# Letting the list of a fused attention and feed-forward kernel place the pooled sums on either of two engines

## The chip, the cores and the metric

The kernel runs on one core of a Trainium2 chip. The metric is the device time of one execution in microseconds (us); lower is better. The engines named below are TensorE (PE, matrix products; PEld is its weight load), VectorE (DVE), ScalarE (ACT), GpSimd (POOL) and SyncE (SP, which issues most DMA transfers). Each engine works through its own instructions in the order in which the program issued them, and an instruction that waits holds back those behind it.

## The reference

Per batch of 8, with 8 heads, 576 tokens and 64 columns a head (float32):

```python
q_d, k_d, v_d = (t.reshape(B, H, S // 4, 4, D).mean(axis=3) for t in (q, k, v))
out_up = np.repeat(softmax(scale * q_d @ k_d.T) @ v_d, 4, axis=2)      # pooled attention
mask = abs(pos[:, None] - pos[None, :]) < 4
out_local = softmax(where(mask, scale * q @ k.T, -1e9)) @ v            # local attention
x = (out_up + out_local).transpose(0, 2, 1, 3).reshape(B, S, H * D)
xn = (x - mean) / sqrt(var + 1e-6) * g_ln                              # over 512 columns
out = x + relu(xn @ w_ch1) @ w_ch2                                     # 512 -> 2048 -> 512
```

The weights come as 64-bit floats.

## The kernel before

**Feed-forward part.** The 4608 tokens are cut into 9 chunks of 512. TensorE visits every chunk twice: in the first stage with 5 of 8 pairs of weight columns (`wide`, L1228, and `down`, L1299), in the second with the other 3 (`product`, L1218, and `down`). Every operand is split into a high and a low part (`halved`: ScalarE copies the high part, L407; VectorE subtracts, L413), and three products make one of full precision. Between the two products ScalarE takes the ReLU (L1236) and VectorE the low rest (`hl`, L1243 and L1285), which also frees the PSUM bank of the first product.

**Attention part.** It runs beside the first stage. For each batch `pooled(b)` makes two halves of four heads (number i = 2b + half). For q, k and v of a half there are two loads into a staging tile (`raw4q` is q of i = 4; L819 on SP's queue; only 2 staging tiles, `NSTG`) and a sum of four tokens by two additions in `pool4` (L832 over 72x512 and L833 over 72x256). Batch 0 has its own path. After the sums TensorE transposes (`turn_qk`, L880), ScalarE copies (L889, L893), TensorE makes the scores (L907), VectorE the row maxima (L911, L912), ScalarE the exponentials (L920), TensorE transposes them (L926) and multiplies by v (L943), VectorE divides (L962), and `keep` (L968) writes the result to a DRAM tile `ud` by two DMAs from GpSimd's queue. The local attention works on 40 windows (`local`, L553 to L788), whose q and k loads (L566) are issued by SP or, for later windows, by ScalarE. `norm(i)` then adds both: `plus` (L1026) is two DMAs from GpSimd's queue that read `ud` and add into the window's tile `xl`; then VectorE takes the statistics (`stats`, L1049), GpSimd the inverse root (L1055), VectorE normalizes (L1059), GpSimd writes `xl` to DRAM (L1096), TensorE transposes (L1067), and ScalarE scales (L1090).

**Order.** Nothing of this order is fixed by hand. Each step is a task of `Plan` with an engine, a duration, what it depends on, a due time and the buffers that it takes and gives back. `Plan.order` builds one list: it repeatedly takes, over all engines, the task that can start first, within 0.5 us the one due first. A task may have a second engine (`alt`) with a duration and an added wait. The instructions are issued in the list's order, so the list decides what stands ahead of what on every engine. An error of the list's times is no error of the result: the chip's waits still hold, but an instruction that stands too early in its engine's queue blocks those behind it.

For a task that depends on a DMA task the list knows a landing time (`t.lag`). It is added to the time at which the later task may start only under this condition:

```python
x.open = max(x.open, t.end + (t.lag if t.eng == "SP" or set(x.opts) != {t.eng} else 0.0))
```

So it is not added where both tasks are on GpSimd alone, which holds for `keep` followed by `plus`. `plus` has 2 * 0.56 = 1.12 us in the list. `G1` is the gap in due time between the four pairs of heads of batch 1's pooled attention; from batch 2 on the gap is `ROUND / NPAIR`. Until the first product, idle slots of TensorE are filled with dummy products (L216).

Of the kernel before, what the change touches and what calls it, by code (L numbers as in the profile page):

```python
# [22 lines left out]
class Plan:  # L23
# [18 lines left out]
    def add(self, eng, dur, fn, deps=(), due=0.0, take=(), give=(), lag=None, ahead=1e9, alt=None, kb=0, n=1, more=0.1, late=None):  # L42

        opts = {eng: (dur, fn, 0.0)}
        if alt is not None:
            opts[alt[0]] = alt[1:]
        t = SimpleNamespace(
            n=len(self.tasks), opts=opts, dur=dur, deps=[d for d in deps if d is not None],
            due=due, take=take, give=give, lag=lag, ahead=ahead, open=0.0, waits=0, eng=None, fn=None, kb=kb, pieces=n, more=more,
            late=late if late is not None else self.late if eng == "SP" else 0.0,  # L50
        )
        self.tasks.append(t)
        return t

    def order(self):
# [40 lines left out]
        while left:  # L96
# [48 lines left out]
                free[room] = sorted(free[room] + [t.end + t.lag] * n)  # L145
            for x in then.get(t.n, ()):
                x.waits -= 1
                x.open = max(x.open, t.end + (t.lag if t.eng == "SP" or set(x.opts) != {t.eng} else 0.0))
                if not x.waits:
                    for e in x.opts:  # L150
                        ready[e].append(x)
# [6 lines left out]
def attention_then_ffn(  # L158
# [159 lines left out]
    AHEAD = 45  # L318
    U_SPARE = 4
    NEARLY, EARLY = 2, 0  # L320
    G1 = 6
    W2_LATER = 7.0
    W_LEAD = 4.0
    HALT = 1.0
# [13 lines left out]
    def act(n, sbuf=False):  # L338
        return (0.155 if sbuf else 0.14) + n / 1430.0
# [212 lines left out]
    def local(i):  # L552
# [44 lines left out]
        for src, nm in () if own else ((q, "q"), (k, "k")):  # L597
            if by_pe:

                def turn(nm=nm):  # L600
                    p = psa(f"l{nm}{i}")
                    x.p[nm] = p
                    for pr in range(NPAIR):
                        nc.tensor.transpose(
                            p[:, pr * P : (pr + 1) * P],
                            x.raw[nm][:, 2 * pr : 2 * pr + 2].rearrange("p h d -> p (h d)"), ident,
                        )

                def turn_out(nm=nm):
                    t = unit([P, NPAIR, P], f"l{nm}t{i}")  # L610
                    nc.scalar.copy(t.rearrange("p c t -> p (c t)"), x.p[nm])
                    setattr(x, nm + "t", t)

                t = add("SP", 1.33, lambda src=src, nm=nm: load_rows(src, nm), (), due - 12.0, take=U,
                        lag=LAT, kb=360, n=2, more=1.0, ahead=AHEAD)
                t = add("PE", 0.43, turn, (t,), due - 8.0, take=A, give=U)
                turned.append(add("ACT", act(512), turn_out, (t,), due - 8.0, take=U, give=A))
            else:

                def turn(nm=nm):  # L620
                    t = unit([P, H, 64], f"l{nm}t{i}")
                    nc.vector.transpose(
                        t.rearrange("p h j -> p (h j)"), x.raw[nm].rearrange("p h j d -> p (h j d)")
                    )
                    setattr(x, nm + "t", t)

                ts = []
                for jb in range(2):
                    ts.append(add("SP", 2.0, lambda src=src, nm=nm, jb=jb: load_blocks(src, nm, jb, nc.sync), ts,
                                  due - 14.0, take=() if jb else U, lag=LAT, kb=200, n=4, more=0.8, ahead=AHEAD,  # L630
                                  alt=("ACT", 3.2, lambda src=src, nm=nm, jb=jb: load_blocks(src, nm, jb, nc.scalar), LATER) if i >= ALSO else None))
                turned.append(add("DVE", dve(512), turn, ts, due - 8.0, take=U, give=U))
        if own:

# [146 lines left out]
        for h2 in range(2):  # L781
            t = add("DVE", 0.28, lambda h2=h2: inverse(h2), (tv,), due)
            outs.append(
                add("DVE", dve(256) * (1 if by_pe else 2), lambda h2=h2: divided(h2, "DVE"), [t] + outs, due,
                    take=() if h2 else U, give=A,
                    alt=("ACT", (4 if by_pe else 8) * act(64), lambda h2=h2: divided(h2, "ACT"), 0))
            )
        local_out[i] = x, outs  # L788

# [11 lines left out]
    def pooled_half(b, hg):  # L801
# [8 lines left out]
        for nm, src in (("v", v),) if own else (("q", q), ("k", k), ("v", v)):  # L810
            for half in range(2):
                key = (nm, half)
                due = pooled_at(b, 2 * hg) - (8.0 if nm == "v" else 14.0)

                def load(src=src, key=key):
                    half = key[1]
                    raw = work.tile([P, 1024], F32, tag="stg", bufs=NSTG, name=f"raw{i}{key[0]}{half}")
                    raw = raw[:GH].rearrange("p (h e) -> p h e", h=4)
                    nc.sync.dma_start(  # L819
                        raw,  # L820
                        src[b, 4 * hg : 4 * hg + 4, half * S // 2 : (half + 1) * S // 2, :]
                        .rearrange("h (g r) d -> g h (r d)", r=FACTOR),
# [13 lines left out]
                if own:  # L836
# [23 lines left out]
                    "DVE" if by_dve else "POOL", dve(512) + dve(256) if by_dve else 2.1,  # L860
                    (lambda key=key: pool4(key, nc.vector)) if by_dve else pool4, [t, lastg.vd[hg] if nm == "v" else None] + ready.get(nm, []),
                    due, take=U if half == 0 and nm != "v" else (), give=STG,
                )
                ready.setdefault(nm, []).append(t)
        for pr in range(2):
# [147 lines left out]
    def norm(i):  # L1013
# [88 lines left out]
            lastup["own"] = t  # L1102
            t = kept = add("DVE", dve(512), keep_x, [t] + outs, due - 1.0, give=A)
        else:
            t = kept = add("POOL", 2 * BEGUN, plus, ud_done[b] + outs, due - 4.0, lag=LAT, kb=400, n=2, more=0.6)
        t = add("DVE", 1.1, stats, (t,), due - 1.0)
        t = add("POOL", 0.52, rstd, (t,), due - 1.0)
        t = add("DVE", 0.46, normed, (t,), due, take=U, ahead=12.0)
# [357 lines left out]
```

## Time and profile before

| | us |
|---|---|
| median of 3 runs | 1030.08 |
| lowest and highest | 1027.56, 1035.27 |
| the profiled execution | 1034.97 |
| its span, first to last instruction | 1033.2 |
| mean granted TensorE clock in it | 0.997 of 2.4 GHz |

The profiled execution is one of its own and lies near the upper end of the runs; 1.8 us of its time lie outside the span. Start times below are from the start of the span. In brackets behind an instruction stands how long its engine had been idle before it, and what ended that.

### The profile page before, as it was taken

The page shows a single profiled execution, that of the slowest core. Times are in us where ns is not written, and L with a number is a line of the kernel's source. Part 1 is how long each engine was busy: PE and PEld are TensorE (multiplying, and loading weights), DVE is VectorE, ACT ScalarE, POOL GpSimd, SP SyncE. Part 2 cuts the span into 40 slices and gives each one's busy share as a digit, 9 for nine tenths or more (in the row PEclk, how much of TensorE's full clock was granted, in tenths as well). Part 3 has the DMA queues.
Part 4 walks back from the last instruction along what each step waited for, and adds up shares of the span by engine and source line. Part 5 has one row for each costly group of instructions (what it writes and reads, how often), then busy time and mean ns, then how long its engine had stood idle before and what let it go on. Part 6 is the DMA issues. An engine that isn't in the chain of part 4 may idle for free. (4 is left out here: it accounts for less than half of the span.)

```text
span 1033.2 us, 23017 instructions
## 1 busy us (share of the span) xinstructions
PE 1010.6 (98%) x8322; PEld 854.0 (83%) x8322; DVE 664.5 (64%) x1562; ACT 446.2 (43%) x1396; POOL 482.2 (47%) x573
## 2 busy tenths in 40 slices
PE   9999999998999899999999999999999999999998
PEld 8788888787887788778888887888888999989897
DVE  6898987775665455476656644573595676557743
ACT  6587655353363354353352453553342233322311
POOL 4463696674766575574652232351254213333112
PEclk9999999999999999999999999999999999999999
DMA  7899898897888678677577233441245422444313
GB/s 177 223 288 229 201 209 198 172 222 160 180 177 186 150 190 159 144 188 159 131 163 141 66 110 86 127 153 41 88 157 183 164 89 94 146 163 164 113 65 108
DMA packets 272785, 159.23 MB, mean 154 GB/s; under 512 B 196032, under 2 KB 241344, under 8 KB 272672
## 3 DMA queue, kind: packets, MB, share of 16 engines
q1 hardware_dynamic: 243456, 110.68, 43.4%
q0 software_dynamic: 18336, 45.77, 16.1%
q10 hardware_dynamic: 10880, 1.31, 0.9%
q8 instruction: 66, 1.08, 0.5%
q14 instruction: 47, 0.39, 0.1%
HBM read 111.68 MB, written 46.01 MB: 153 GB/s over the span
## 5 line engine op out<-in xcount | busy, mean ns | idle before, releaser
L1299 PE MATMUL acc<-hiw,hl 128*128 128x512 f32 x576 | 233.9, 406 | 0.0
L1299 PE MATMUL acc<-low,hh 128*128 128x512 f32 x576 | 225.9, 392 | 0.0
L1299 PE MATMUL acc<-hiw,hh 128*128 128x512 f32 x576 | 225.4, 391 | 0.0
L1299 PEld LDWEIGHTS acc<-hiw,hh 128*128 128x128 f32 x576 | 108.4, 188 | 24.0
L1381 POOL TENSOR_TENSOR back<-back,back 128x512 f32<-128x512 f32 x36 | 48.2, 1351 | 171.0 <-DMA back<-parts 148.4
L1299 PEld LDWEIGHTS acc<-hiw,hl 128*128 128x128 f32 x576 | 108.6, 189 | 19.8
L1299 PEld LDWEIGHTS acc<-low,hh 128*128 128x128 f32 x576 | 108.9, 189 | 18.0 <-DVE low L413 0.4
L1236 ACT ACTIVATE hh<-h 128x256 fp32r<-128x256 f32 x180 | 59.4, 388 | 143.7 <-PE h L1228 129.2
L1228 PE MATMUL h<-hix,hiw 128*128 128x512 f32 x360 | 110.6, 402 | 0.0
L1243 DVE SCALAR_TENSOR_TENSOR hl<-h,hh 128x256 fp32r<-128x256 f32 x180 | 67.3, 414 | 63.3 <-ACT hh L1236 52.2
L1228 PE MATMUL h<-hix,low 128*128 128x512 f32 x360 | 103.4, 408 | 1.3 <-DVE low L413 0.9
L1279 ACT ACTIVATE hh<-e 128x256 fp32r<-128x256 f32 x108 | 39.0, 410 | 146.0 <-DVE e L1260 78.4
L1228 PE MATMUL h<-lox,hiw 128*128 128x512 f32 x360 | 97.0, 391 | 0.0
L1026 POOL DMA_DIRECT2D xl<-ud x70 | 60.6, 1108 | 64.2 <-DVE xl L754 16.8
L1228 PEld LDWEIGHTS h<-lox,hiw 128*128 128x128 f32 x360 | 67.7, 188 | 15.1
L1228 PEld LDWEIGHTS h<-hix,low 128*128 128x128 f32 x360 | 64.7, 190 | 15.3 <-DVE low L413 1.6
L1228 PEld LDWEIGHTS h<-hix,hiw 128*128 128x128 f32 x360 | 65.5, 190 | 13.1
L1090 ACT ACTIVATE xg<-px,gain 128x58 f32<-128x58 f32 (+15 forms) x280 | 61.6, 371 | 9.3 <-PE px L1067 9.2
L1260 DVE TENSOR_TENSOR e<-h,s 128x512 f32<-128x512 f32 x27 | 18.7, 691 | 68.8 <-PE h L1218 54.8
L1285 DVE SCALAR_TENSOR_TENSOR hl<-e,hh 128x256 fp32r<-128x256 f32 x108 | 55.4, 566 | 4.9 <-PE acc L1299 3.6
L1055 POOL TENSOR_TENSOR mv<-mv,neg_half 128x1 f32<-128x1 f32 x40 | 24.8, 621 | 71.0 <-DVE mv L1052 71.0
L1049 DVE BATCH_NORM_STATS2 st<-xl 128x6 f32<-128x512 f32 x40 | 27.5, 687 | 42.1 <-DMA xl<-ud 37.4
(247 smaller groups left out, 2101.7 us busy)
## 6 DMA issues: line engine op xcount, KB each, us to landing
s<-in_moe_w_ch_dram SPq DMA_DIRECT2D x64, 256.0 KB
blocks<-xg POOLq DMA_DIRECT2D x36, 256.0 KB, 4.4
parts<-part POOLq DMA_DIRECT2D x36, 256.0 KB, 3.3
xf_B<-blocks SPq DMA_DIRECT2D x36, 256.0 KB
back<-xs SPq DMA_DIRECT2D x36, 256.0 KB
back<-parts SPq DMA_DIRECT2D x36, 256.0 KB
out_dram<-back SPq DMA_DIRECT2D x36, 256.0 KB
xl<-ud POOLq DMA_DIRECT2D x70, 128.0 KB, 4.5
```

What stands on the lines that cost most here:

```text
L1026: nc.gpsimd.dma_start(xl()[hs], ud[b][t0 : t0 + 64], accum_op=ALU.add)
L1049: nc.vector.bn_stats(st, xl())
L1055: nc.gpsimd.tensor_tensor(x.mv[:, 1:2], x.mv[:, 1:2], neg_half, op=ALU.pow)
L1090: nc.scalar.activation(to, at, AF.Copy, scale=gain[:, kc : kc + 1])
L1228: nc.tensor.matmul(y.ps[fi], lhsT=wt[a][:, kc * P : (kc + 1) * P], rhs=xx[b], start=n == 0, stop=n == 3 * KC - 1)
L1236: nc.scalar.activation(hh[v, p, th][:, 256 * fi : 256 * fi + 256], side(fi, th), AF.Relu)
L1243: nc.vector.scalar_tensor_tensor(out=hl[v, p, th][:, fs], in0=side(fi, th), scalar=0.0, in1=hh[v, p, th][:, fs].bitcast(F32), op0=ALU.max, ...
L1260: nc.vector.tensor_add(two(y.e1), two(y.ps[1]), both(y.s))
L1279: nc.scalar.activation(hh[v, p, th][:, 256 * fi : 256 * fi + 256], place(th, fi), AF.Relu)
L1285: eng.scalar_tensor_tensor(out=hl[v, p, th][:, fs], in0=place(th, fi), scalar=0.0, in1=hh[v, p, th][:, fs].bitcast(F32), op0=ALU.max, op1= ...
L1299: nc.tensor.matmul(acc[v, th][j], lhsT=lt[:, ts], rhs=rt, start=p == 0 and fi == 0 and n == 0, stop=p == npr - 1 and fi == 1 and n == 2,)
L1381: nc.gpsimd.tensor_add(y.x, y.x, y.p)
```

## The change

Three things in the list's data and one in its rule. The sums of pooled attention of batches 2 to 7 get VectorE as a second engine, with 0.93 us of duration (two additions, by the same function `dve`) and an added wait of 1.0 us; GpSimd's figure stays 2.1 us. A landing time is now counted behind every task that moves data (`t.kb`). `plus` is put down with 1.9 in place of 1.12 us. `G1` goes from 6 to 3 us. `alt` becomes a list; `load` gets an argument for the engine, which nobody passes.

```diff
         opts = {eng: (dur, fn, 0.0)}
-        if alt is not None:
-            opts[alt[0]] = alt[1:]
+        for a in alt or ():
+            opts[a[0]] = a[1:]
...
-                x.open = max(x.open, t.end + (t.lag if t.eng == "SP" or set(x.opts) != {t.eng} else 0.0))
+                x.open = max(x.open, t.end + (t.lag if t.kb or t.eng == "SP" or set(x.opts) != {t.eng} else 0.0))
...
-    G1 = 6
+    G1 = 3
...
-                def load(src=src, key=key):
+                def load(src=src, key=key, eng=nc.sync):
...
-                    nc.sync.dma_start(
+                    eng.dma_start(
...
                     due, take=U if half == 0 and nm != "v" else (), give=STG,
+                    alt=[("DVE", dve(512) + dve(256), lambda pool4=pool4: pool4(eng=nc.vector), 1.0)] if b > 1 else [],
...
-            t = kept = add("POOL", 2 * BEGUN, plus, ud_done[b] + outs, due - 4.0, lag=LAT, kb=400, n=2, more=0.6)
+            t = kept = add("POOL", 1.9, plus, ud_done[b] + outs, due - 4.0, lag=LAT, kb=400, n=2, more=0.6)
```

## Rows read from the trace of the kernel before

**Rows 1.** The page's busy time by engine: us, share of the span, instructions.
```profile
PE 1010.6 (98%) x8322; PEld 854.0 (83%) x8322; DVE 664.5 (64%) x1562; ACT 446.2 (43%) x1396; POOL 482.2 (47%) x573
```

**Rows 2.** Busy time in two stretches, the one with attention and the rest: stretch, length, busy us of each engine (instructions), granted clock, DMA share, GB/s.
```profile
100.00:600.00 500.00, 487.06 (x4353) 399.69 (x4353) 322.67 (x863) 226.62 (x770) 299.97 (x373) 0.99 0.76 168
600.00:1033.20 433.20, 428.79 (x2668) 375.17 (x2667) 259.02 (x487) 147.44 (x394) 134.97 (x129) 1.00 0.36 121
```

**Rows 3.** What TensorE waited for from 100 to 600 us, the three largest: us in total, times, longest.
```profile
PE gs L907 <- ACT ktg L893: 3.3, 1, 3.3
PE ls L676 <- DVE hl L1243: 3.1, 1, 3.1
PE gq L880 <- POOL kd L833: 2.3, 1, 2.3
```

**Rows 4.** The timeline of all engines from 335 to 352 us.
```profile
335.13 1.48 POOL L968 DMA_DIRECT2D ud<-od  x2
...
342.31 1.78 POOL L1026 DMA_DIRECT2D xl<-ud  x2 [3.57 <-DMA ud<-od]
...
348.50 0.69 DVE L1049 BATCH_NORM_STATS2 st<-xl 128x6 f32<-128x512 f32 x1 [7.52 <-DMA xl<-ud]
...
351.02 0.68 PE L676 MATMUL ls<-lkt,lqt 64*64 64x64 f32 x28 [3.07 <-DVE hl L1243]
```

**Rows 5.** The timeline of all engines from 425 to 444 us.
```profile
431.92 1.78 POOL L1026 DMA_DIRECT2D xl<-ud  x2 [5.08 <-DMA ud<-od]
...
438.34 0.69 DVE L1049 BATCH_NORM_STATS2 st<-xl 128x6 f32<-128x512 f32 x1 [6.48 <-DMA xl<-ud]
...
440.22 0.70 PE L732 MATMUL lv<-vwin,at 64*64 64x65 f32 x32 [1.29 <-issue]
...
440.66 1.93 DVE L912 TENSOR_SCALAR gmx<-gmx 96x3 f32<-96x3 f32 x1
...
441.25 1.30 POOL L832 TENSOR_TENSOR raw13v<-raw13v 72x512 f32<-72x512 f32 x1
...
443.13 1.06 PE L926 MATMUL gt<-ident,ag 96*72 96x96 f32 x6 [0.64 <-ACT ag L920]
```

**Rows 6.** Busy time and granted clock (the third number from the end) behind two of TensorE's waits; columns as in Rows 2.
```profile
239.00:243.00 4.00, 4.00 (x18) 3.49 (x17) 2.75 (x8) 3.02 (x11) 0.00 (x0) 0.57 0.68 146
351.00:356.00 5.00, 4.98 (x40) 4.00 (x41) 3.25 (x12) 3.36 (x12) 4.26 (x6) 0.66 0.45 80
```

**Rows 7.** The timeline of all engines from 188 to 197 us.
```profile
188.93 5.09 POOL L1026 DMA_DIRECT2D xl<-ud  x6 [1.65 <-PE h L1228]
...
192.45 2.86 POOL L832 TENSOR_TENSOR raw6k<-raw6k 72x512 f32<-72x512 f32 x1
...
195.39 0.72 POOL L833 TENSOR_TENSOR kd<-raw6k 72x256 f32<-72x256 f32 x1
...
196.17 0.28 PE L880 MATMUL gq<-ident,kd 72*128 72x72 f32 x1 [2.28 <-POOL kd L833]
```

**Rows 8.** The timeline of all engines from 230 to 240 us.
```profile
230.85 6.95 ACTq L566 DMA_DIRECT2D qr<-in_q_dram  x4
...
238.75 1.44 PE L907 MATMUL gs<-ktg,qbdg 128*96 128x144 f32 x6 [3.27 <-ACT ktg L893]
```

**Rows 9.** The waits of all engines from 100 to 700 us: us in total, times, longest.
```profile
DVE st L1049 <- DMA xl<-ud: 37.4, 13, 7.5
...
POOL xl L1026 <- DMA ud<-od: 14.4, 4, 5.1
```

**Rows 10.** VectorE's timeline from 480 to 700 us, the one wait of this kind over 3 us in it.
```profile
604.50 0.69 DVE L1049 BATCH_NORM_STATS2 st<-xl 128x6 f32<-128x512 f32 x1 [7.12 <-DMA xl<-ud]
```

**Rows 11.** GpSimd's waits from 107 to 600 us for the loads of the pooled sums of batches 2 to 7: the largest and the smallest of 17 such rows, which together have 37.4 us in 20 waits.
```profile
POOL raw12k L832 <- DMA raw12k<-in_k_dram: 7.0, 1, 7.0
...
POOL raw7q L832 <- DMA raw7q<-in_q_dram: 0.3, 1, 0.3
```

**Rows 12.** GpSimd's busy time in the first additions of the sums of batches 2 to 7 (L832): stretch, length, busy us (instructions), clock, DMA share, GB/s.
```profile
107.00:600.00 493.00, 104.96 (x72) 0.99 0.76 168
```

**Rows 13.** The same for the second additions (L833).
```profile
107.00:600.00 493.00, 54.27 (x72) 0.99 0.76 168
```

**Rows 14.** A VectorE operation of two SBUF inputs, from the instructions of L413: ns min/median/max, first and last start.
```profile
L413 DVE TENSOR_TENSOR loT<-xT,hiT x27: 677/681/730, 696.9 to 977.3; 128x512 fp32r<-128x512 f32 x27
```

**Rows 15.** A VectorE operation over 72x256, from the instructions of L962; columns as in Rows 14.
```profile
L962 DVE TENSOR_TENSOR od<-gv,gr x32: 420/421/422, 26.1 to 594.9; 72x256 f32<-72x256 f32 x32
```

**Rows 16.** A small VectorE operation in SBUF, from the instructions of L912; columns as in Rows 14.
```profile
L912 DVE TENSOR_SCALAR gmx<-gmx x32: 165/166/1926, 17.9 to 586.8; 96x3 f32<-96x3 f32 x32
```

**Rows 17.** `plus` from the instructions of L1026: ns min/median/max of one of its two DMAs.
```profile
L1026 POOL DMA_DIRECT2D xl<-ud x70: 803/926/3025, 122.9 to 659.0; - x70
```

**Rows 18.** The time to landing of `keep`, from the instructions of L968.
```profile
DMA to landing us min/median/max: 3.4/5.0/7.5
```

**Rows 19.** The timeline of all engines from 46 to 65 us: the last scaling, the split and the first product of the first stage.
```profile
57.44 5.29 ACT L1090 ACTIVATE xg<-px,gain 128x116 f32<-128x116 f32 x24 [1.77 <-PE px L1067]
...
62.43 2.36 ACT L407 CAST hix<-xg 128x512 fp32r<-128x512 f32 x4
...
63.28 2.06 PE L1228 MATMUL h<-hix,low 128*128 128x512 f32 x4 [0.20 <-ACT hix L407]
```

**Rows 20.** The waits in SP's queue over the whole span: us in total, times, longest.
```profile
SPq L819 <- POOL qd L833: 22.9, 12, 5.6
```

More of the change, by code (lines that the diff above doesn't have):

```diff
@@ L630, in local @@
                                   due - 14.0, take=() if jb else U, lag=LAT, kb=200, n=4, more=0.8, ahead=AHEAD,
-                                  alt=("ACT", 3.2, lambda src=src, nm=nm, jb=jb: load_blocks(src, nm, jb, nc.scalar), LATER) if i >= ALSO else None))
+                                  alt=[("ACT", 3.2, lambda src=src, nm=nm, jb=jb: load_blocks(src, nm, jb, nc.scalar), LATER)] if i >= ALSO else []))
                 turned.append(add("DVE", dve(512), turn, ts, due - 8.0, take=U, give=U))
@@ L785, in local @@
                     take=() if h2 else U, give=A,
-                    alt=("ACT", (4 if by_pe else 8) * act(64), lambda h2=h2: divided(h2, "ACT"), 0))
+                    alt=[("ACT", (4 if by_pe else 8) * act(64), lambda h2=h2: divided(h2, "ACT"), 0)])
             )
```

## The prediction

> **What bounds the kernel now.** I read the page's busy times first: TensorE is busy for 98% of the span [rows 1], so no other engine's busy time is worth anything by itself; only TensorE's idle time, and what its clock loses behind it, can be won. The table by stretches says where that lies: from 100 to 600 us, where the attention runs beside the first stage, TensorE is idle for 500 - 487.06 = 12.9 us; from 600 us on for 4.4 us, mostly the last output's way out [rows 2]. All that the change moves lies before 600 us. Even if every idle microsecond there went, and the clock loss below with it (3.4 us), the gain would be 16 us, 1.6%. The list of TensorE's waits names the three large ones [rows 3], and the timeline around each shows its cause. There the reader is to follow a wait back to the first instruction that stood in a queue before it could run.
>
> The wait at 348 us (3.07 us) is for a PSUM bank that VectorE's `hl` frees. `hl` stands behind `stats`, which waited 7.52 us for the landing of `plus`; `plus` was issued at 342.31 because GpSimd had stood 3.57 us until the `keep` issued at 335.13 had landed [rows 4]. The same chain ends at 440 and 443 us: GpSimd waits 5.08 for `ud`, VectorE 6.48 for `xl`, TensorE 1.29 and 0.64 [rows 5]. Here the list believed that `plus` could follow `keep` at once; `keep` takes 3.4 to 7.5 us to land [rows 18]. After the longer wait the clock is granted 0.66 of full on average over 5 us, that is part of the time at 1.2 instead of 2.4 GHz, after an idle TensorE [rows 6].
>
> The wait at 194 us (2.28 us) is for a pooled sum: GpSimd was 5.09 us in six `plus` DMAs, then added for k, while TensorE waited [rows 7]. The wait at 235 us (3.27 us) is another matter: ScalarE issued four loads in 6.95 us and the copy that TensorE needs stood behind them [rows 8]. The change gives no direct reason for that one to go.
>
> **The change part by part.**
>
> *The landing time and the 1.9 us of `plus`.* No instruction is added or removed; `stats` and what hangs on it move back in VectorE's queue, and other work of GpSimd moves ahead of `plus`. GpSimd's wait for `ud` is 14.4 us in 4 cases [rows 9], VectorE's for `xl` 37.4 us in 13 [rows 9]. I charge what TensorE lost by them: 3.07 + 1.29 + 0.64 = 5.00 us of idle time [rows 4, 5], and the clock behind the first, 5 us x (1 - 0.66) = 1.70 [rows 6]. Sum 6.70 us. Of the other two `ud` cases one put VectorE behind by 7.12 us and cost TensorE nothing that its wait list shows [rows 10]. The figure of 1.9 is right: two DMAs of 0.926 us at the median make 1.85 [rows 17]. What is late next where these stalls go is the ordinary chain of a window, scores, maxima, exponentials; other products of the stage lie ready there, so I cost it at nothing. If that cover is gone, the same wait comes back a little later, at most with its 5.00 us.
>
> *Sums on VectorE.* 72 sums may move. One costs GpSimd (104.96 + 54.27) / 72 = 2.21 us [rows 12, 13], and by the nearest rows 0.68 + 0.42 = 1.10 us on VectorE, for 512 columns from SBUF and for 256 columns [rows 14, 15]. VectorE is chosen where it can start 1 us earlier than GpSimd. How many that is, the trace cannot show. GpSimd is busy 60% of this stretch (299.97 of 500) [rows 2] and about half of that in pieces that leave over 1 us to wait, so I take a third, 24, with 8 and 48 as the ends. That takes 24 x 2.21 = 53 us off GpSimd and puts 24 x 1.10 = 26 us on VectorE, which goes from 322.67 to 349 of 500 us: still room. On the path this wins the 2.28 us at 194 us [rows 7]. Earlier sums also free the two staging tiles: SP stood 22.9 us behind sums of q alone [rows 20], with the window loads in its queue behind; no wait of TensorE goes back to that, so I count it at nothing, between 0 and a wait like the smallest named, 0.64.
>
> Against it stands a new wait. A sum in VectorE's queue waits there for its load, and `hl`, the maxima and `stats` stand behind it; TensorE waits for their banks. GpSimd's waits for these loads are 37.4 us [rows 11], 0.52 us a sum; 24 sums bring 12.5 us into VectorE's queue. What a microsecond of such standing costs TensorE, the `xl` waits show: 6.70 us lost for 37.4 us waited [rows 9], 0.18. So 12.5 x 0.18 = 2.2 us lost. Ends: 8 sums, 0.7; 48 sums, 4.5. The lower end reaches below nothing: every sum that leaves GpSimd also stops delaying VectorE's small SBUF operations, one of which took 1.93 us beside an addition of GpSimd [rows 5] against 0.166 at the median [rows 16].
>
> That last pair of rows speaks of a port. The Trainium skill says the same and draws a conclusion that is against this change: by its page "SBUF — State Buffer" (section "SBUF: two separate sides") an operation of VectorE with two SBUF inputs and one of GpSimd exclude each other for their whole length, and by "Perfetto Trace Analysis" (section "Optimizing Scalar/DVE Operations") work moved between these two engines might not help. The trace agrees on the exclusion where those two rows lie; on the conclusion no row here decides. The sum above leaves the lock out; with it, the move's gain of 2.28 would be zero or less, as the first rival has it.
>
> *G1.* Batch 1's first three pairs come due 9, 6 and 3 us later, and their loads, 576 KB for the first halves of q and k, may stand behind the window and weight loads of the start. The first stage starts at 63.28 us, held by ScalarE's scaling and split [rows 19], and none of batch 1's work lies in those rows. I take 0, with 2 us either way (the length of the split, 2.36 us [rows 19], is about what could move past it).
>
> **The sum.** Against the profiled execution (1034.97): 6.70 + 2.28 - 2.2 = 6.8 us less, 1028.2. That execution is 4.9 us above the median, and the same list ran in both, so part of its stalls is not in the median; I take half of the 4.9 as belonging to the stalls named, which leaves (8.98 - 2.45) - 2.2 = 4.3 us against the median: 1030.08 - 4.3 = 1025.8. I forecast **1026 us**. A measurement of this kernel, whose three runs span 0.75%, can tell about 1% from no change, so this is a gain on the edge of visibility.
>
> **The rivals.**
>
> *The port makes the move a wash (0.25).* A moved sum holds GpSimd up while it runs and waits itself for GpSimd's additions, up to 1.3 us each (the length of one, rows 5). 24 x 1.3 = 31 us of VectorE at 0.18 is 5.6 us, and the 2.28 is not won. Then 6.70 less the share not in the median (6.70 x 6.5 / 8.98 = 4.9) against between 2.2 and 5.6: 1027.4 to 1030.8, middle 1029. For it: VectorE's 1.93 us in rows 5. Against: the sums that leave GpSimd stretch VectorE in the same way today.
>
> *VectorE stands behind late loads (0.15), the case on the slow side.* One mechanism: the sum enters VectorE's queue where the list expects its load, the load lands later because SP's queue is late, and `hl` stands behind. It decides from 6.5 / 0.18 = 36 us of such waits on; 48 sums with twice GpSimd's wait of 0.52 are 50 us, which cost 9 us: 1030.08 - 6.5 + 9 = 1032.6, and with one clock drop of 1.7 us as in rows 6 for each of two longer stalls 1036. For it: a load was 7.0 us late on GpSimd [rows 11], and 7.52 us on VectorE cost TensorE 4.8 with the clock. Against: GpSimd takes a sum that VectorE has no time for.
>
> *The new order also removes the rest (0.12).* The wait at 235 us goes by the reordering, 3.27 and 4 us x (1 - 0.57) = 1.72 behind it [rows 6, 8], and G1 wins 2 us at the start: 1025.8 - 7.0 = 1019.
>
> *VectorE gets almost no sum (0.08).* Its added 1 us may decide every case for GpSimd, which is idle 40% of the stretch. Then only the landing times act: 1030.08 - 4.9 = 1025, which the time cannot tell from the forecast, though the instruction counts by engine can.
>
> **How the numbers follow.** The forecast itself has 0.40, with 1022 to 1030 from the ends of its terms (G1 2, the loads 1.5 up or 2.3 down, the share of the median). The range takes in the wash whole, the bold reordering down to 1018 and the slow case up to 1035, leaving about 2 in 10 outside. Faster by over 1% means under 1019.8: half of the reordering case and the tails of two others, 0.13. Slower by over 1% means over 1040.4, only the far end of the slow case, 0.05. Within 1%: 0.82.
>
> **What the changed profile would show.** Right: GpSimd no longer waits for `ud` ahead of `plus` (14.4 us before), VectorE's wait for `xl` well under 37.4 us, 8 to 48 pairs of additions of L832 and L833 on VectorE at 0.68 and 0.42 us each, TensorE's idle time from 100 to 600 us near 8 us instead of 12.9, and no granted clock under 0.7 there except behind a wait of ScalarE's loads. Wrong: a wait of VectorE's L832 for its load of over 3 us with `hl` behind it, additions on VectorE that last 1.5 us or more, or the same idle time of TensorE in other places. The number fails most simply if the list, in changing everywhere, puts a step too early that today stands well; nothing in the trace of before can show that.

## The result and the profile after

The changed kernel takes 1044.14 us (median of 4, 1042.18 to 1045.46) beside 1030.09 for the kernel before (median of 4 in the same comparison): a ratio of 1.0128, 95% interval 1.0086 to 1.0171. I had forecast 1026 within 1018 to 1035, with 0.05 for slower by over 1%. Direction and size were both wrong. The profiled execution of after took 1043.84 us, that of before 1034.97: the traces hold 8.9 us of the 14 us between the medians, and where the other 5 us lie no trace shows. Its lines stand one lower than those of before from L862 on (`plus` L1027, `stats` L1050, `hl` L1244, and so on).

The two stretches of [rows 2] in after, columns as there:

```profile
100.00:600.00 500.00, 483.33 (x4317) 397.17 (x4316) 316.42 (x860) 230.90 (x792) 290.34 (x362) 0.98 0.74 165
600.00:1033.00 433.00, 433.00 (x2726) 379.22 (x2725) 257.15 (x498) 146.33 (x389) 136.90 (x134) 1.00 0.37 121
```

TensorE is idle for 500 - 483.33 = 16.7 us in the attention stretch, where it was 12.9 [rows 2] and I expected 8. From 600 to 1033 us it has no idle microsecond; the loss was made before that. What the 16.7 us waited for, the four largest of after's TensorE waits (total, times, longest):

```profile
PE gs L908 <- ACT ktg L894: 4.6, 1, 4.6
PE lv L732 <- ACT at L718: 4.5, 1, 4.5
PE gt L927 <- DVE hl L1244: 3.7, 1, 3.7
PE h L1229 <- DVE low L413: 2.0, 1, 2.0
```

Set beside [rows 3], the stalls over 2 us are as many in this stretch, three, but each is longer, none stands at an old place, and the fourth lies ahead of 100 us. After's timeline from 258 to 267 us has the first:

```profile
259.93 6.12 ACTq L566 DMA_DIRECT2D kr<-in_k_dram  x4
...
266.09 0.56 ACT L890 COPY qbdg<-gq 64x144 f32<-64x144 f32 x2 [9.67 <-DMA kr<-in_k_dram]
...
266.99 1.76 PE L908 MATMUL gs<-ktg,qbdg 128*96 128x144 f32 x6 [4.63 <-ACT ktg L894]
```

The list gave ScalarE four window loads to issue and put the copy that TensorE needs behind them. From the first issue to the end of the last it is 6.12 us, where the list counts 3.2. That is the mechanism of [rows 8], at another window. The second, from 306 to 320 us:

```profile
306.52 9.28 ACTq L566 DMA_DIRECT2D qr<-in_q_dram  x4
...
315.86 1.21 ACT L1237 ACTIVATE hh<-h 128x256 fp32r<-128x256 f32 x4 [10.81 <-DMA qr<-in_q_dram]
...
317.65 0.71 DVE L622 STREAM_TRANSPOSE lqt<-qr 128x512 f32<-128x512 f32 x1 [6.79 <-DMA kr<-in_k_dram]
...
318.28 2.04 DVE L1244 SCALAR_TENSOR_TENSOR hl<-h,hh 128x256 fp32r<-128x256 f32 x6
...
319.14 0.68 PE L927 MATMUL gt<-ident,ag 96*72 96x96 f32 x6 [3.73 <-DVE hl L1244]
```

Here two queues are held at once. ScalarE's four loads hold it for 9.28 us, and VectorE's transposition of the window's q (L622) stands 6.79 us with the six `hl` behind it, on which TensorE's PSUM banks depend. An issue by itself is short. From the instructions of L566 in after (ns min/median/max of one):

```profile
L566 ACTq DMA_DIRECT2D qr<-in_q_dram x20: 318/352/1776, 183.3 to 391.2; - x20
```

The four at 306 us start at 306.52, 308.35, 311.23 and 315.49 and last 0.32 to 0.33 us each. So the time lies between them, up to 3.9 us from the end of one to the next, and no wait is shown there. The third stall, from 435 to 449 us:

```profile
440.28 4.64 SPq L566 DMA_DIRECT2D kr<-in_k_dram  x4
...
445.24 0.69 DVE L1050 BATCH_NORM_STATS2 st<-xl 128x6 f32<-128x512 f32 x1 [3.62 <-DMA xl<-ud]
...
446.01 0.58 ACT L718 COPY at<-lt 128x512 f32<-128x512 f32 x1 [7.00 <-DMA parts<-part]
...
446.65 1.25 PE L732 MATMUL lv<-vwin,at 64*64 64x65 f32 x32 [4.50 <-ACT at L718]
```

ScalarE's copy `at` takes its buffer from the same pool as `part`, and waits until the write of a `part` has landed: 7.00 us of waiting, while four window loads take 4.64 us to be issued and VectorE waits for `plus`.

Behind each of these four stalls the granted clock falls. Windows laid on the stretches of 1.2 GHz, after's four and then before's two (the third number from the end is the granted clock):

```profile
97.80:101.20 3.40, 3.40 (x16) 2.71 (x15) 3.37 (x7) 2.43 (x8) 1.53 (x2) 0.50 0.95 231
265.00:271.80 6.80, 4.81 (x43) 3.98 (x44) 2.77 (x8) 4.21 (x16) 4.76 (x6) 0.50 0.83 149
319.70:323.10 3.40, 3.40 (x12) 2.81 (x11) 1.56 (x5) 2.16 (x5) 0.78 (x2) 0.50 0.68 165
445.90:452.70 6.80, 6.05 (x47) 5.00 (x48) 3.05 (x12) 2.84 (x8) 3.51 (x6) 0.50 0.43 78
```

```profile
239.10:242.50 3.40, 3.40 (x15) 3.00 (x14) 2.75 (x8) 2.92 (x11) 0.00 (x0) 0.50 0.67 142
351.80:355.20 3.40, 3.40 (x9) 2.66 (x10) 2.52 (x8) 2.81 (x10) 2.92 (x5) 0.50 0.35 79
```

After is busy for 3.40 + 4.81 + 3.40 + 6.05 = 17.66 us at half clock, which would cost 8.8 us if all that time had been twice too long; before 6.80, which would cost 3.4. So the account is 16.7 - 12.9 = 3.8 us of idle time, 2.0 us of the stall at 95 us, and 8.8 - 3.4 = 5.4 us of clock: 11.2 us. The two profiled spans differ by 1042.1 - 1033.2 = 8.9 us; the account overshoots it by 2.3 us. The overshoot lies in the clock's term. Over the whole span TensorE's idle time grew from 22.6 to 29.0 us, its dummy products took 20.3 and 19.7 us, and everything else that it computed took 990.3 and 993.4: only 3.1 of the 5.4 us show as longer work.

What the change itself was to do can be read too. Waits on all engines from 100 to 700 us, the one row of after that is left of [rows 9]:

```profile
DVE st L1050 <- DMA xl<-ud: 29.0, 15, 4.2
```

GpSimd's 14.4 us for `ud` have no row any more (0.3 us in one wait are left). And the first additions of a sum on VectorE, from the instructions of L832 in after (ns min/median/max, first and last start), are these alone:

```profile
L832 DVE TENSOR_TENSOR raw9k<-raw9k x1: 686/686/686, 284.4 to 284.4; 72x512 f32<-72x512 f32 x1
L832 DVE TENSOR_TENSOR raw12k<-raw12k x1: 644/644/644, 380.5 to 380.5; 72x512 f32<-72x512 f32 x1
```

Two sums of 72 moved, not 24; their second additions (L833) take 0.42 us each. The wait at 194 us [rows 7] is gone as well, though the sum that it waited for stayed on GpSimd: the new order removed it, not the move.

### The profile page after: what moved, and what is told of

It reads as the page before. It is cut to its first block, busy times and chain, and to the rows that moved or that the text cites. A ratio compares the mean times of both kernels' runs of the same rounds, so it can differ in the third digit from the quotient of the medians.

```text
span 1042.1 us, 23019 instructions
## 1 busy us (share of the span) xinstructions
PE 1013.1 (97%) x8314; PEld 856.5 (82%) x8314; DVE 659.5 (63%) x1565; ACT 445.5 (43%) x1400; POOL 475.4 (46%) x569
## 3 DMA queue, kind: packets, MB, share of 16 engines
q1 hardware_dynamic: 243456, 110.68, 42.6%
## 4 chain that ended last, share of the span: by engine, by line
PE 78%; DMA 10%; DVE 4%; SPq 2%; issue 2%; ACT 1%; POOL 1%; DVEq 0%; POOLq 0%; ACTq 0%
PE acc L1300 34%; PE h L1229 17%; PE h L1219 13%; DMA qr<-in_q_dram 2%; PE gv L944 2%; SPq L566 2%; DMA vwin<-in_v_dram 2%; PE lv L732 2%; PE gs L908 2%; DMA kr<-in_k_dram 2%; PE lt L711 1%; PE ls L676 1%; PE px L1068 1%; PE gt L927 1%; DMA s<-in_moe_w_ch_dram 1%
## 5 line engine op out<-in xcount | busy, mean ns | idle before, releaser
L1237 ACT ACTIVATE hh<-h 128x256 fp32r<-128x256 f32 x180 | 59.7, 388 | 145.3 <-PE h L1229 118.2
L1244 DVE SCALAR_TENSOR_TENSOR hl<-h,hh 128x256 fp32r<-128x256 f32 x180 | 67.2, 415 | 64.2 <-ACT hh L1237 59.7
L1027 POOL DMA_DIRECT2D xl<-ud x70 | 60.6, 1109 | 51.4 <-DVE xl L754 21.8
L1097 POOL DMA_DIRECT2D xs<-xl x80 | 48.0, 633 | 1.7 <-issue 1.7
```

What stands on the lines that cost most here:

```text
L1027: nc.gpsimd.dma_start(xl()[hs], ud[b][t0 : t0 + 64], accum_op=ALU.add)
L1097: nc.gpsimd.dma_start(xs[q0 : q0 + n], xl()[r0 : r0 + n])
L1237: nc.scalar.activation(hh[v, p, th][:, 256 * fi : 256 * fi + 256], side(fi, th), AF.Relu)
L1244: nc.vector.scalar_tensor_tensor(out=hl[v, p, th][:, fs], in0=side(fi, th), scalar=0.0, in1=hh[v, p, th][:, fs].bitcast(F32), op0=ALU.max, ...
```

## The experiments

All ratios are against the kernel before on the same chip (its median was 1031 to 1033 us there), with 95% intervals. They are the record's, and can differ a little from the quotient of two medians, most for the kernel with `plus` at 1.12 us (1038.27 beside 1032.72 would be 1.0054).

**One part undone at a time.** First theory: one of the four edits brings the loss. Rival: the loss belongs to the list as a whole.

```diff
-    G1 = 3
+    G1 = 6
```


> The changed kernel with G1 back at 6; everything else as changed. Theory A (one part carries the loss): if it is G1, which shifts batch 1's loads and sums into the start of the stage, the time returns to 1030 to 1034 and TensorE's wait of 2.0 us near 95 us goes; if not, it stays at 1042 to 1046. Theory B (any edit to the list's data reorders everything and the time is decided by where a few long waits of TensorE happen to fall): somewhere from 1026 to 1045, with waits of over 3 us at other places than in the changed kernel, and a time that is no sum of parts.

Measured: 1036.12 us, 1.0034 (1.0008 to 1.0061). The stalls at 262, 315 and 442 us are gone, and TensorE waits for the weight's low part at 95 us for 0.4 us at most. ScalarE still stands for 8.26 us behind four window loads, from 257.91 us on and ahead of the same copy, but here TensorE waits only 1.16 us for it: 6.12 us of a held queue cost 4.63 in one order, 8.26 cost 1.16 in the other.

```profile
100.00:600.00 500.00, 489.90 (x4401) 401.49 (x4400) 322.38 (x867) 232.07 (x799) 293.73 (x366) 0.99 0.76 169
```

```diff
-                    alt=[("DVE", dve(512) + dve(256), lambda pool4=pool4: pool4(eng=nc.vector), 1.0)] if b > 1 else [],
```


> The changed kernel with GpSimd as the sums' only engine. Only 2 of 72 sums moved to VectorE in the changed kernel, some 2.2 us of VectorE's time in all, so by the work moved alone the time stays at 1042 to 1046. Theory A for this part (the second engine also adds 0.6 us to the list's view of every sum that follows a sum, and so delays what hangs on them): back to 1030 to 1034. Theory B: anywhere from 1026 to 1045, other places of the long waits.

Measured: 1043.07, 1.0101 (1.0032 to 1.017). The TensorE waits of this kernel are after's own, line for line (lines as in before here):

```profile
PE gs L907 <- ACT ktg L893: 4.5, 1, 4.5
PE gt L926 <- DVE hl L1243: 3.2, 1, 3.2
PE lv L732 <- ACT at L718: 3.0, 1, 3.0
```

So the choice of engine, which gives the change its name, is not the cause: without it the same three stalls stand.

```diff
-                x.open = max(x.open, t.end + (t.lag if t.kb or t.eng == "SP" or set(x.opts) != {t.eng} else 0.0))
+                x.open = max(x.open, t.end + (t.lag if t.eng == "SP" or set(x.opts) != {t.eng} else 0.0))
```


> The changed kernel with the old condition for the landing time. If the prediction's chain was right, GpSimd again waits some 10 to 15 us for ud ahead of plus, VectorE some 37 us instead of 29 for xl, and the time rises by 3 to 7 us, to 1047 to 1051. Theory A for this part (the later start of plus is what harms): 1030 to 1034. Theory B: from 1026 to 1045.

Measured: 1041.31, 1.009 (1.0058 to 1.0123). The time did not rise as the prediction's chain would have it. GpSimd stands for `ud` again, VectorE's waits for `xl` are 30.2 us where after has 29.0, so their fall from 37.4 in after does not need the landing time, and TensorE's largest waits are new ones:

```profile
POOL xl L1027 <- DMA ud<-od: 10.6, 5, 3.1
```
```profile
PE px L1068 <- DVE xn L1060: 3.8, 1, 3.8
PE gq L881 <- DMA kr<-in_k_dram: 3.2, 1, 3.2
```

```diff
-            t = kept = add("POOL", 1.9, plus, ud_done[b] + outs, due - 4.0, lag=LAT, kb=400, n=2, more=0.6)
+            t = kept = add("POOL", 2 * BEGUN, plus, ud_done[b] + outs, due - 4.0, lag=LAT, kb=400, n=2, more=0.6)
```


> The changed kernel with plus at 1.12 us in the list. It changes no instruction's own cost; by its truth it is worth 0.7 us in GpSimd's order for each of 35 windows. Theory A for this part: 1030 to 1034. Theory B: from 1026 to 1045 with long waits of TensorE elsewhere. If all four runs of this call lie within 3 us of the changed kernel, none of the parts alone carries the loss and theory B is wrong too, since they reorder the list without effect.

Measured: 1038.27, 1.0036 (1.0007 to 1.0065).

Undoing G1 gives back 0.94% of 1.28, undoing the 1.9 us 0.92, the landing 0.38 and the engine choice 0.27 (these two within their intervals). These add up to 2.5%, twice the loss, though with four such intervals the sum is not clear of 1.28. But two parts that have nothing to do with each other each give back most of it, so none of them is its cause alone.

**The parts alone, on the kernel before.** If the parts add, those alone make 1.28% together.

```diff
-    G1 = 6
+    G1 = 3
```


> The kernel before with G1 = 3 alone. 457 of TensorE's 4600 instructions change places, the first at about 46 us. Theory A (G1 carries the loss): ratio to the kernel before 1.006 to 1.013. Theory B (the list is scattered by any edit, and the time of a new list is a draw): anywhere from 0.995 to 1.013. By what undoing it in the changed kernel gave (1.0128 to 1.0034): 1.009.

Measured: 1034.4, 1.0028 (0.9994 to 1.0062).

```diff
-            t = kept = add("POOL", 2 * BEGUN, plus, ud_done[b] + outs, due - 4.0, lag=LAT, kb=400, n=2, more=0.6)
+            t = kept = add("POOL", 1.9, plus, ud_done[b] + outs, due - 4.0, lag=LAT, kb=400, n=2, more=0.6)
```


> The kernel before with plus at 1.9 us alone; 310 of TensorE's instructions change places. Theory A for this part: 1.006 to 1.013. Theory B: anywhere from 0.995 to 1.013. If the parts added up, G1 alone, the landing time alone (1.000) and this would make 1.0128 together.

Measured: 1033.77, 1.002 (0.9991 to 1.0048).

The landing time alone, the term of my sum on which most rested:

```diff
-                x.open = max(x.open, t.end + (t.lag if t.eng == "SP" or set(x.opts) != {t.eng} else 0.0))
+                x.open = max(x.open, t.end + (t.lag if t.kb or t.eng == "SP" or set(x.opts) != {t.eng} else 0.0))
```


> The kernel before with the landing time counted behind every task that moves data, nothing else of the change. The prediction's main term: the waits of GpSimd for ud (14.4 us) go, TensorE's waits at 348 and 440 us with them, 4.9 us less than the kernel before, ratio 0.993 to 0.997. Theory B (the edit reorders everything, the time is decided by where other waits fall): GpSimd's wait for ud goes just the same, but the ratio lies anywhere from 0.995 to 1.013.

Measured: 1031.61, 0.9998 (0.9973 to 1.0024). Its waits for `ud` and `xl`, and the largest of TensorE:

```profile
DVE st L1049 <- DMA xl<-ud: 21.2, 13, 3.7
POOL xl L1026 <- DMA ud<-od: 2.8, 1, 2.8
```
```profile
PE lv L732 <- issue: 4.0, 1, 4.0
```

Both waits fell as I predicted (37.4 to 21.2, 14.4 to 2.8), and the stalls at 348 and 440 us went. The time did not move: a stall of 3.97 us stands from 267 to 271 us instead, for which the profile names no releaser. Beside it VectorE stood 8.34 us for a window's load, `hl` followed at 270.04, and TensorE went on at 270.85; that it waited for `hl` is read from this order:

```profile
269.40 0.71 DVE L622 STREAM_TRANSPOSE lqt<-qr 128x512 f32<-128x512 f32 x1 [8.34 <-DMA qr<-in_q_dram]
```

The sums on VectorE, moved at their place with the list untouched:

```diff
-                    nm, half = key
+                    (nm, half), eng = key, nc.vector if b > 1 and (i + key[1] + "qkv".index(key[0])) % 3 == 0 else eng
```


> The kernel before, its list's order untouched, but every third of the 72 sums of batches 2 to 7 (24) is computed by VectorE at its place in the list. It prices the move that the prediction sized and the changed kernel hardly makes (2 sums). By the prediction's terms: 2.2 us lost in waits for loads in VectorE's queue, some of the 2.3 us at 194 us won, so the ratio is 0.997 to 1.003 and the additions last 0.68 and 0.42 us. By the port rival: additions of 1.5 us and more, ratio 1.000 to 1.006. By the rival of late loads: VectorE waits 12 us and more for loads with the ReLU's rest behind, ratio above 1.006.

Measured: 1032.04, 1.0001 (0.9977 to 1.0025). The first additions from 107 to 600 us, busy us of VectorE and GpSimd (instructions), and the two waits of VectorE ahead of them that are for loads of the sums:

```profile
107.00:600.00 493.00, 16.31 (x24) 68.31 (x48) 0.99 0.76 168
```
```profile
  DMA raw13k<-in_k_dram: 3.8, 1
  DMA raw10k<-in_k_dram: 1.6, 1
```

24 first additions at 16.31 / 24 = 0.68 us each, as estimated from [rows 14]; and 5.4 us of waits (7.7 with two others) where I had 12.5. And no gain or loss that shows: the 53 us that GpSimd is spared are no wait of TensorE's. This says little of the port: only 3 of the 24 met a computation of GpSimd, for under 0.6 us each, and none met one of its first additions.

Alone the parts give 0.28, 0.20 and -0.02%, each below the loss with its whole interval, and 24 moved sums 0.01. Together the edits give 1.28. They do not add, as far as these intervals tell; the choice of engine alone, on the kernel before, was not run.

**How far lists scatter.** Two edits with no meaning for the hardware: the planner's tie window and one of its spacings.

```diff
-        self.hold = 0.5
+        self.hold = 0.52
```


> The kernel before with the list's tie window at 0.52 in place of 0.50 us, an edit without a meaning of its own; 460 of TensorE's instructions change places, as many as with G1 = 3. Theory A (the change's parts have a harm of their own): within 0.3% of the kernel before. Theory B: a draw like the others, off by 0.3 to 1.3%, more likely slower than faster, since the kernel before is a list that was picked.

```diff
-    W_NORM, G_NORM = 2.0, 9.0
+    W_NORM, G_NORM = 2.1, 9.0
```


> The kernel before with the due times of the windows 0.1 us earlier, again without a meaning of its own; 396 of TensorE's instructions change places. Theory A: within 0.3% of the kernel before. Theory B: off by 0.3 to 1.3%, more likely slower.

Measured: 1049.31, 1.018 (1.0136 to 1.0224), and 1031.64, 1.0003 (0.9984 to 1.0022).

A tie window wider by 0.02 us costs no less than the whole change. A ratio of 1.0128 for a new list is therefore within what a new list alone can do. The second kernel also warns against reading idle time as time lost: TensorE is idle for 6.1 us from 100 to 600 us there, half of before's 12.9, and the time is the same; its busy time over the span is 1015.8 us where before has 1010.6.

**Whether ScalarE's issuing is the cause.** Two of after's three stalls stand behind loads on ScalarE. Here after's list is kept, and those loads are issued from SP's queue at the same place of the list:

```diff
-                                  alt=[("ACT", 3.2, lambda src=src, nm=nm, jb=jb: load_blocks(src, nm, jb, nc.scalar), LATER)] if i >= ALSO else []))
+                                  alt=[("ACT", 3.2, lambda src=src, nm=nm, jb=jb: load_blocks(src, nm, jb, nc.sync), LATER)] if i >= ALSO else []))
```


> The changed kernel's list, order untouched on TensorE, VectorE and GpSimd; the ten groups of four window loads that ScalarE issued are issued by SP at the same place of the list. Theory C (the changed kernel loses in its new order because ScalarE stands in a load issue of 6.1 us at 260 us and 9.3 us at 306 us while TensorE needs the copy or the ReLU behind it): TensorE's waits of 4.6 us at 262 us and 3.7 us at 315 us go, with 3.4 and 1.7 us of half clock behind them, so the time falls by 8 to 13 us, to 1031 to 1036 (ratio to the kernel before 1.000 to 1.005). Theory D (those loads are late in any case, the transfers hold everything up): SP's queue is only longer, the waits stay, 1042 to 1050.

Measured: 1046.53, 1.014 (1.0086 to 1.0194). ScalarE's stalls are gone and others came:

```profile
PE gq L881 <- POOL kd L833: 6.7, 3, 4.3
PE gv L944 <- POOL vd L833: 3.9, 2, 2.4
```

The same edit on the kernel before:

> The same edit on the kernel before, order untouched. Theory C: its wait of 3.3 us at 235 us, behind 6.95 us of load issue on ScalarE, goes with 1.7 us of half clock: 1025 to 1029, ratio 0.995 to 0.999. Theory D: 1030 to 1038.

Measured: 1036.04, 1.0041 (1.0011 to 1.0071). The wait at 235 us [rows 8] went, and did not pay. The engine that issues is not the cause: what the loads lose on ScalarE they lose on SP, where the loads of the pooled sums stand behind them. GpSimd's waits for those loads, from 100 to 600 us, rise from 65.0 to 74.4 us in after's list and from 45.9 to 71.6 in before's.

**Whether it is the window loads at all.** After's VectorE waits ahead of L622, by releaser, then those of before:

```profile
  DMA kr<-in_k_dram: 20.8, 6
  DMA qr<-in_q_dram: 12.8, 7
  DMA raw7v<-in_v_dram: 4.0, 1
```
```profile
  DMA kr<-in_k_dram: 11.9, 7
  DMA qr<-in_q_dram: 4.6, 3
```

37.6 us where before has 16.5. Among after and its variants this wait goes roughly with the time (9.5 us at 1.0034, 21.7 at 1.0036, 29.6 at 1.009, 41.1 at 1.0101, 44.0 at 1.014), but the kernel with the landing time alone has 36.6 and loses nothing, before with its loads on SP has 37.0 and loses 0.41%, and the list with the wider tie window has 21.1 and loses 1.8%, so the wait is no price by itself. The next three kernels make the loads lighter instead: from window 9 on q and k come in 2 transfers of 256-byte rows instead of 8 of 128-byte rows, the same bytes. The blocks then lie as the scores can't use them, so these kernels leave out the right local attention of those windows and show the schedule alone.

```diff
-            for par in range(2):
-                t0 = window_start(w, par) + 32 * jb
-                for dh in range(2):
-                    i0 = 64 * par + 32 * dh
+            for par in range(2 - 2 * jb):
+                t0 = window_start(w, par)
+                for dh in range(1):
+                    i0 = 64 * par
...
-                        x.raw[nm][i0 : i0 + 32, :, jb, :],
-                        src[b, :, t0 : t0 + 32, 32 * dh : 32 * dh + 32].rearrange("h c d -> c h d"),
+                        x.raw[nm][i0 : i0 + 64].rearrange("p h j d -> p h (j d)"),
+                        src[b, :, t0 : t0 + 64, :].rearrange("h c d -> c h d"),
```


> The kernel before with its order untouched on TensorE, VectorE and GpSimd, but the q and k loads of windows 9 to 39 made with 2 transfers in place of 8 and rows of 256 in place of 128 bytes; all of a tensor is loaded where its first half was. The same bytes, a quarter of the issues, half the packets; the layout is not the one that the scores need, so the local attention of these windows is not computed rightly. Theory D (new and old lists differ in time by how their steps meet loads that come later than the list believes): 10 to 15 us less, ratio 0.985 to 0.992, TensorE's idle time from 70 to 700 us under 7 us instead of 13. Theory F (the order of the compute steps alone makes the waits): ratio 0.995 to 1.002.

> The same edit on the changed kernel, order untouched; the local attention is again not computed rightly. Theory D: the gap to the kernel before, 1.3%, closes to under 0.4% of the same edit on the kernel before, so the ratio to the kernel before is 0.986 to 0.995. Theory F: the gap stays, ratio 1.006 to 1.013, and the waits at 262, 315 and 442 us stand.

Measured: before with row loads 1029.87, 0.998 (0.9949 to 1.0011); after with row loads 1024.63, 0.9939 (0.9913 to 0.9965). For after this is in the range of theory D and outside that of F. For before it is not: the gain of 10 to 15 us that D expected did not come, and 0.998 lies in F's range. Its ten runs spread from 1023.17 to 1035.71, and the profiled one (1024.39) is the second fastest. The stretch of attention in before's and in after's list, and in after's list the two places where its worst stalls had been:

```profile
100.00:600.00 500.00, 495.33 (x4469) 407.14 (x4468) 329.99 (x875) 234.12 (x799) 306.50 (x379) 1.00 0.71 170
```
```profile
100.00:600.00 500.00, 493.94 (x4490) 407.08 (x4488) 324.64 (x881) 237.48 (x817) 302.22 (x375) 1.00 0.70 169
...
260.00:275.00 15.00, 15.00 (x147) 12.47 (x140) 11.74 (x34) 6.76 (x23) 11.22 (x15) 1.00 0.67 169
435.00:455.00 20.00, 20.00 (x170) 16.52 (x169) 12.07 (x32) 11.93 (x46) 12.87 (x19) 1.00 0.69 186
```

With the lighter loads VectorE waits for no window load ahead of L622 in either kernel, and TensorE is idle 4.7 us in before's list and 6.1 in after's. After's stalls at 262 and 442 us are gone with their half clock, and its list is no longer slower. The 1.28% are thus what this list loses by meeting the window loads as they are, not something in the list that stands whatever they do. The edit changes four things at once (fewer transfers to issue, longer rows, less time on the DMA engines, and the second half of a tensor loaded already with the first), and which of them does it I did not separate. Nor does it touch these loads alone: GpSimd's waits for the loads of the pooled sums fall with it from 65.0 to 24.7 us in after's list, so what the window loads do to the loads behind them is part of the 1.28%.

The page's row of the hardware queue bears on the third of these: from after to after with row loads it goes from 243456 packets and 42.6% of 1042.1 us to 177504 and 40.5% of 1023.6, that is from 444 to 415 us of all 16 engines. The Trainium skill, "DMA: Bandwidth & Descriptors", section "Why small descriptors are slow (HBM only)", says that each packet carries a fixed overhead that weighs more the shorter it is; that agrees in direction with these two rows.

> The same edit on the list with the tie window of 0.52 us, which was 1.8% slower than the kernel before; order untouched, the local attention not computed rightly. Theory D: ratio to the kernel before 0.987 to 0.998, within 0.5% of the other two of this call. Theory F: 1.010 to 1.018.

Measured: 1041.82, 1.0121 (1.0072 to 1.017). The list with the wider tie window stays slow, as theory F has it, and its largest wait of TensorE is for a pooled sum:

```profile
PE gq L880 <- POOL kd L833: 3.1, 1, 3.1
```

So the window loads explain after, and not every slow list. This one loses its time earlier. Its TensorE computes dummy products where before's has none (L216 from 120 to 160 us, before and then the list with the wider tie window, with its own loads; they are not confined to the time ahead of the first product, before's last is at 117.8 us):

```profile
120.00:160.00 40.00, 0.00 (x0) 1.00 0.95 210
120.00:160.00 40.00, 8.60 (x60) 0.96 0.78 166
```

By 160 us TensorE has done 147.0 - 28.8 = 118.2 us of other work there, and 153.6 - 20.3 = 133.3 in before; these 15 us are nearly all of the 15.5 by which the two spans differ (1048.7 and 1033.2). With row loads 12 of 17 us are lost by then. The planner puts dummy products where its own list leaves TensorE idle, so 8.6 of these us fill gaps that the list itself plans and that can be read from it without a run. Why the tie window opens them, and what the rest is, stays open.

No kernel that computes the whole of the reference was clearly faster than the kernel before.

## Why the prediction was wrong

The forecast was 1026, the result 1044. In the order of the working: the term that should have won most won nothing that shows, and the sum has no term at all for what lost the time, the new order meeting window loads that come late. With lighter window loads after takes 1024.63 beside 1029.87 for before.

**Right: the waits that the landing time removes.** GpSimd's wait for `ud` fell from 14.4 us to 0.3 in after and to 2.8 with that edit alone, and the stalls of [rows 4, 5] went in both.

**Wrong, the first step that failed: "other products of the stage lie ready there, so I cost it at nothing."** The term was 6.70 us in the profiled execution, 4.9 against the median. With that edit alone it measured 0.2 us of 1032, with 2.6 either way. I had taken the stalls of before as a debt that a truthful listing pays. But moving `plus` moves what stands behind it on every queue, and another step found its data late: 3.07 us at 348 went and 3.97 at 267 came, beside a wait of 8.34 us for a window's load. That explains a term of 5 us that came to nothing. The 14 us lost by the whole change are the step behind it, the same assumption of cover made for the whole new order: the three stalls of 4.63, 3.73 and 4.50 us with their half clock, which go when the window loads are lighter.

**Wrong: the number of sums.** 2 moved where I took 24 with ends of 8 and 48. The rival with a chance of 0.08 is what happened to the sums, not to the time; that the added 1 us decides nearly every case for GpSimd is its reason, and no run changed that figure. The price of a sum was right (0.69 + 0.42 against 1.10). Of its worth nothing can be seen: with 24 really moved, the 2.28 us to be won and the 2.2 us to be lost came to 0.1 us slower together, with 2.5 either way. The wait that was to go at 194 us is 1.50 us there instead of 2.28, and its sum was not among the moved. That the net was near the forecast is no support for either part.

**Wrong beside the other edits: G1 at nothing, with 2 us either way.** Alone it costs 2.9 us (0.6 less than nothing to 6.4), which does not refute the term. Undoing it in after gives back 9.7 (1044.14 against 1.0034 x 1030.9). I looked for its effect in the start of the first stage, and the first product begins only 0.6 us later (63.92 against 63.28). It acts through the order of what follows. The one direct trace of it is at 95 us, where the wait of 2.03 us is 0.4 with G1 back at 6. After's timeline:

```profile
91.01 3.40 DVE L387 SCALAR_TENSOR_TENSOR cva<-s,cva 128x256 int32<-128x256 int32 x2
...
91.86 1.39 POOL L832 TENSOR_TENSOR raw3k<-raw3k 72x512 f32<-72x512 f32 x1
...
97.10 1.51 PE L1229 MATMUL h<-hix,low 128*128 128x512 f32 x4 [2.03 <-DVE low L413]
```

A sum of batch 1 lies beside VectorE's unpacking of a weight, two operations that last 0.42 us each at the median and here 3.40 together (the first 2.53), and TensorE stands 2.03 us for the weight's low part.

**The rivals.** The port as the price of moved sums did not show: 24 of them ran at 0.68 us. But they hardly met GpSimd's computations, so this list did not put the port to the test. The Trainium skill's rule that I weighed there ("SBUF — State Buffer", section "SBUF: two separate sides") agrees with the row at 91 us, where both inputs of L387 lie in SBUF; the operation of [rows 5] that I had set beside it has only one. Its conclusion ("Perfetto Trace Analysis", section "Optimizing Scalar/DVE Operations") agrees with the ratio of 1.0001, though not by way of the lock. VectorE behind late loads of the sums, my slow case, did not occur: no sum on VectorE waited in after. Late loads did hold VectorE, those of the windows, which I had not priced at all; the row of that kind in before ([rows 8], 6.95 us on ScalarE) I had set aside as one that "the change gives no direct reason" to move.

**Wrong: the clock.** I charged 1.70 us once, as won. After pays up to 8.8 where before pays up to 3.4: behind its stalls of 4.5 us stand 6.8 us at half clock, behind those of 2 to 4 us at most 3.4.

**The range.** It allowed each step its own error and none to the list. The last sentence of the prediction named that failure, "puts a step too early that today stands well", and gave it no chance and no price. The two meaningless edits would have given a first measure of both: +1.8% and 0. That the bounds of the terms missed the result is no bad luck, since none of the errors that I gave the terms reaches 18 us.

## What to carry to other kernels

Where a planner makes the whole order, measure first what meaningless edits of it do to the time; a change whose own terms are smaller than that scatter can't be forecast from them, and a single run can't credit it either. Look first at what the list itself shows, here dummy products where it leaves TensorE idle. Paying off a named wait was worth nothing here because something else in the same stretch was late: look how many other waits stand beside it (here the window loads, 16.5 us of VectorE's waiting) before costing what comes next at nothing. A correct cost put into the list for one step gained nothing while a larger error of the list, loads that leave and land late, stayed in it.

## What the runs showed of the hardware that I had not expected

- Four loads that ScalarE issues hold it for up to 9.28 us, of which the issues themselves are 1.3 (four of 0.32 or 0.33). What holds the rest no row says. The DMA engines were busy for 0.93 of the time there (306 to 316 us), and for 0.80 where it was 6.12 us (259 to 267 us).
- TensorE idle for 4.63 and 4.50 us was followed by 6.80 us at 1.2 GHz; idle for 2.03, 3.07, 3.27 and 3.73 us by 3.40 us; idle for 2.28 us ([rows 7]) by none (granted clock 1.00 from 196.4 to 200.0 us).
- Two integer operations of VectorE with two inputs from SBUF took 3.40 us instead of 0.84 beside GpSimd's two additions of a sum (91.01 to 94.41 us in after). The 24 additions that were moved to VectorE took 0.65 to 0.69 us, with hardly a computation of GpSimd beside them.
- The write of a `part` landed so late that the buffer's next user waited 7.00 us, though the median to landing is 3.4 us for this transfer in the same run (2.3 to 7.1).
